# Infini-attention scores on one core: q and k as two fp32r parts, even and odd heads in the two row halves of the array, scores of two heads nine apart issued together

## The chip, the cores and the metric

The kernel runs on one core of a Trainium2 chip. The metric is device time in microseconds (us). TensorE (PE) has a row of its own in the profile for loading its stationary operand (PEld); DVE is VectorE, ACT is ScalarE, POOL is GpSimd, SP is SyncE, which issues most transfers (POOL issues a few).

## The reference

Two independent parts are computed and put side by side. Part A is attention with a compressive memory: 2048 tokens of 576 numbers, 32 heads of 18, in four segments of 512 tokens. Part B is a spectral filter: a 2-D FFT of a 2048 x 576 array, a product with complex weights, and the way back.

```python
q,k,v = x@wq, x@wk, x@wv            # 32 heads of 18, 4 segments of 512
for s in range(4):
    logits = qs @ ks.T * 18**-.5 + mask     # mask: -1e9 where the query is before the key (row < col)
    a_dot = softmax(logits) @ vs
    pq = phi(qs)                            # t+1 or exp(t)
    a_mem = (pq @ M) / (pq @ z + 1e-6)      # M, z: sums over earlier segments
    outs.append(g*a_mem + (1-g)*a_dot)      # g = sigmoid(beta), by head
    M += phi(ks).T @ vs;  z += phi(ks).sum(over tokens)
y_a = concat(outs) @ wo
y_b = irfft2(rfft2(xb) * (w_r + 1j*w_i))
```

## The kernel before

The order of work is written out by hand: Python generators are advanced step by step, and the instructions stand on each engine in the order in which the generators were advanced. The stages follow each other, with some overlap: forward transform of part B, projections, inverse transform, attention.

**Projections** (`projections`, `qk_unit`, `v_unit`). For each of four groups g of 512 tokens (a segment) there are nine units of 128 rows of q and k and four of v. A q/k unit is 14 fp32r matmuls of 512 columns into a PSUM bank pj (line 464). The result leaves as three bf16 parts in a tile sp3: ACT copies the first (line 477), DVE subtracts it from the bank (484), ACT copies the second (488); the third is a DVE subtraction (490) in 18 units, and in the other 18 a matmul with `nid`, the negative identity, takes the second part off inside the bank (492) and ACT copies the rest (493). One transfer per unit stores the tile to qkD in memory (494). Between the units, `pace` inserts butterflies of the transform of part B on DVE; ACT also makes phi of q and k (480, 481), PE transposes it, and sums M and z come from it and v.

**Stacks** (`stack_dmas`). Eight heads of one group make a block n (16 blocks). For each block six transfers bring q parts to a tile Qs (ring of three) and six k parts to a tile Ks (ring of four): 18 rows each, six pieces one under the other. The contraction over these 108 rows is the sum of the six products of parts that matter. The first slot of either ring lies in a tile named x0, which the profile calls x.

**Attention** (`attention`). Its loop has one step t for each of 128 heads. Step t makes the first pass s1 of head t+10 and the second pass s2 of head t. s1 computes the scores with queries as rows, four matmuls for the lower triangle and one with the tile tri that adds the mask, in three banks of the ring s1 (three buffers); DVE takes maxima of them (line 654 and twice line 648). Every four heads `mpath` turns the maxima into rows 108 and 109 of Qs (transpose on PE into mt, ACT copy, a POOL transfer). s2 computes the scores again with keys as rows, now over 110 rows so that the maximum is subtracted, in three banks of the ring s2 (three buffers), and ACT takes the exponential to tiles P. POOL zeroes the triangle of P every four heads (701). Then `pv` (718) multiplies P of four heads by v and a column of ones, four heads beside each other in 32-column groups of the array, in every second step. PSUM has two more banks: pv, and post for the side products.

**Side products** in the same loop: pd (denominators of the memory part, `den`), pn (phi(q) times M, `mem1`), pb (spreading of reciprocals over rows, `mem1` and `combine`) and po (the projection with wo, `oproj`, 15 matmuls in two halves). All take their bank by `bank`:

```python
a="post" if s.now<119 else "s1" if s.now<131 or name=="po" else "s2"
```

They are advanced from one queue `bg` by `run_bg`, at a rate that depends on t modulo 4. `mixed` weaves the combination of group g-1 with the memory part of group g. The functions as they stand before:

## Time and profile before

| | us |
|---|---|
| median of three runs | 712.41 (711.06 to 712.87) |
| span of the profiled execution | 709.2 |
| PE busy | 676.4 |
| PE weight loads busy | 498.7 |
| DVE busy | 556.2 |
| ACT busy | 441.0 |
| POOL busy | 208.8 |

The profiled execution is known by its span, from the first to the last instruction; the runs' median is 3.2 us above it. Busy time is the union of an engine's instructions. Ends of matmuls are modelled, so that they overlap in the list; starts are what tells how fast PE goes. A product of plain f32 operands (pv, pn, pd) shows as two records.

### The profile page before, as it was taken

How to read it: one execution, taken by the hardware profiler on the slowest of the kernel's cores; microseconds unless marked ns; L12 is line 12 of the kernel's file. 1: busy time of each engine (PE TensorE's matmuls, PEld its weight loads, DVE VectorE, ACT ScalarE, POOL GpSimd, SP SyncE). 2: the span in 40 equal slices, each digit the busy share in tenths (PEclk: the TensorE clock that was granted, in tenths of full speed). 3: DMA queues.
4: the chain of work that ended last, by engine and by line, in shares of the span. 5: the costliest groups of instructions: out<-in, count | busy, mean ns of one | idle time of the engine just before them, and what ended most of it. 6: DMA issues, size and time to landing. Idle time of an engine off the chain costs nothing.

```text
span 709.2 us, 14168 instructions
## 1 busy us (share of the span) xinstructions
PE 676.4 (95%) x4861; PEld 498.7 (70%) x4861; DVE 556.2 (78%) x1233; ACT 441.0 (62%) x994; POOL 208.8 (29%) x409
## 2 busy tenths in 40 slices
PE   4999999999999999999999899999999999998997
PEld 4999779889879888999844444444566445764677
DVE  6999999899989889887588688877666876568153
ACT  3657695574574563444388677777666676567741
POOL 2110000100100111565165334555233753246210
PEclk9999999999999999999999999999999999999999
DMA  9876546555563568899647666676556765441331
GB/s 343 272 233 205 150 141 194 175 178 167 165 211 133 165 215 279 201 239 211 180 109 176 172 161 154 173 181 169 128 129 185 171 164 128 122 129 52 99 100 69
DMA packets 83388, 121.04 MB, mean 171 GB/s; under 512 B 11368, under 2 KB 50902, under 8 KB 83180
## 3 DMA queue, kind: packets, MB, share of 16 engines
q1 hardware_dynamic: 76724, 104.11, 51.8%
q0 software_dynamic: 6592, 16.03, 8.2%
q8 instruction: 38, 0.62, 0.4%
q14 instruction: 34, 0.28, 0.1%
HBM read 81.78 MB, written 38.24 MB: 169 GB/s over the span
## 4 chain that ended last, share of the span: by engine, by line
PE 61%; DVE 9%; DMA 6%; ACT 5%; issue 3%; POOL 3%; DVEq 0%; SPq 0%; ACTq 0%; POOLq 0%
PE pv L718 9%; PE po L861 7%; PE pj L464 6%; PE pjv L464 6%; PE s L644 5%; PE i L300 4%; PE i L311 4%; PE s L652 3%; PE s L688 3%; PE po L892 2%; DVE junk L648 2%; PE s L692 2%; PE pn L791 2%; PE pm L524 2%; PE s L653 2%
## 5 line engine op out<-in xcount | busy, mean ns | idle before, releaser
L648 DVE CUSTOM_DVE_ANT_0 junk<-s,mask 128x512 bf16<-128x512 f32 (+1 forms) x256 | 141.8, 554 | 55.1 <-PE s L644 44.3
L654 DVE TENSOR_REDUCE mx<-s 128x4 f32<-128x512 f32 x128 | 87.9, 687 | 20.0 <-PE s L653 18.2
L689 ACT ACTIVATE P<-s 128x512 f32<-128x512 f32 x128 | 77.2, 603 | 24.1 <-PE s L688 20.9
L718 PE MATMUL pv<-P,vs 128*32 128x512 f32 (+3 forms) x1024 | 82.3, 440 | 0.0
L694 ACT ACTIVATE P<-s 128x512 f32<-128x512 f32 x128 | 77.1, 602 | 6.9 <-PE s L693 3.8
L698 ACT ACTIVATE P<-s 128x256 f32<-128x256 f32 x128 | 49.6, 387 | 49.7 <-PE s L697 49.6
L701 POOL TENSOR_SCALAR_AFFINE_SELECT P<-P 128x512 f32<-128x512 f32 x116 | 69.4, 635 | 5.6 <-ACT P L689 4.7
L718 PEld LDWEIGHTS pv<-P,vs 128*32 128x32 f32 x1024 | 26.9, 109 | 45.0 <-issue 42.9
L464 PE MATMUL pj<-x,wqkh 128*128 128x512 f32 x162 | 56.1, 407 | 0.0
L210 DVE TENSOR_TENSOR t<-Z 128x580 f32<-128x580 f32 x64 | 46.7, 757 | 0.2
L514 POOL MEMSET vt<- 128x32 f32 x16 | 2.4, 159 | 148.8 <-PE pm L524 121.5
L210 DVE TENSOR_TENSOR Z<-t 128x580 f32<-128x580 f32 x64 | 45.9, 756 | 0.0
L644 PE MATMUL s<-Ks,Qs 108*128 108x512 bf16 (+1 forms) x128 | 42.2, 330 | 0.0
L488 ACT CAST sp<-pj 128x512 bf16<-128x512 f32 x36 | 21.1, 585 | 30.7 <-DVE pj L484 30.7
L142 PE MATMUL f<-ftab,eh 128*128 128x290 f32 (+1 forms) x160 | 31.6, 317 | 9.0 <-DMA ftab<-ftab 9.0
L300 PE MATMUL i<-civ,Y 128*128 128x256 f32 (+1 forms) x288 | 37.9, 284 | 1.6 <-DVE T L332 1.6
L300 PEld LDWEIGHTS i<-civ,Y 128*128 128x128 f32 (+1 forms) x288 | 35.8, 181 | 1.8 <-DVE T L332 1.8
L311 PE MATMUL i<-itab,T 128*128 128x290 f32 (+1 forms) x224 | 36.4, 312 | 0.0
L464 PEld LDWEIGHTS pj<-x,wqkh 128*128 128x128 f32 x162 | 30.4, 188 | 8.4 <-issue 1.7
L669 POOL CAST mh<-mg 128x16 bf16<-128x16 f32 x32 | 6.8, 214 | 99.1 <-ACT mg L667 67.9
L464 PE MATMUL pj<-xh,wqkh 128*128 128x512 f32 x90 | 35.6, 395 | 0.0
L464 PE MATMUL pj<-xh,wqkl 128*128 128x512 f32 x90 | 35.6, 395 | 0.0
(214 smaller groups left out, 1859.6 us busy)
## 6 DMA issues: line engine op xcount, KB each, us to landing
qkD<-sp SPq DMA_DIRECT2D x36, 384.0 KB
Ks<-qkD SPq DMA_DIRECT2D x72, 144.0 KB
x<-qkD SPq DMA_DIRECT2D x60, 144.0 KB
Qs<-qkD SPq DMA_DIRECT2D x60, 144.0 KB
xin<-xb SPq DMA_DIRECT2D x16, 384.0 KB
cfw<-cfw POOLq DMA_DIRECT2D x16, 384.0 KB, 4.5
civ<-civ POOLq DMA_DIRECT2D x16, 384.0 KB, 7.5
vs<-vD SPq DMA_DIRECT2D x16, 330.0 KB
```

Source lines behind the costliest of these rows:

```text
L210: v.tensor_tensor(o,a,b,op=op)
L300: nc.tensor.matmul(p[:m,k],Y[i][:,q,c*128:c*128+m],cc[:,hl,o:o+256],start=n==0,stop=n==5)
L311: nc.tensor.matmul(p,x,t,start=n==0,stop=n==6)
L464: s.nc.tensor.matmul(out,a,b,start=i==0,stop=i==len(L)-1)
L644: nc.tensor.matmul(out,Q[:108,h,128*i:128*i+128],K[:108,h,:128*(i+1)],start=True,stop=True)
L648: nc.vector.tensor_tensor_reduce(out=junk[:,:w],in0=src,in1=s.mask[:,512-w:],scale=1.0,scalar=-3.0e38, op0=OP.add,op1=OP.max,accum_out=s.m ...
L654: nc.vector.tensor_reduce(out=s.mx[k][:,hh],in_=pa.rearrange("p (b c) -> p b c",c=128),axis=mybir.AxisListType.X,op=OP.max)
L689: nc.scalar.activation(P[0][:,hh],p0,AF.Exp,scale=SC)
L694: nc.scalar.activation(P[1][:,hh],p1,AF.Exp,scale=SC)
L701: if k<29: nc.gpsimd.affine_select(out=x,in_=x,pattern=pat+[[1,128]],compare_op=OP.is_ge,fill=0.0,base=0,channel_multiplier=-1)
L718: nc.tensor.matmul(s.pvt[32*hh:32*hh+32,128*j:],vt[:,j,19*h:19*h+32],mv[0][:,hh,mv[1]],start=j==0,stop=j==2,skip_group_check=True)
L861: nc.tensor.matmul(ps,a[t][:r,c],b[:r,t,w],start=i==0,stop=i==14)
```

## The change

1. A q/k unit leaves as two fp32r parts of 4 bytes, hi (an ACT copy) and lo (a DVE subtraction into SBUF). The matmul with nid, the third part and the second ACT copy go; each part is stored by a transfer of its own. hi shares the buffers of v's output tile (tag hv, three of them), and lo has three.
2. A stack holds four heads in rows 0 to 53 and four in rows 64 to 117: even heads in the lower half of the array's rows, odd heads in the upper. Three products (hi hi, hi lo, lo hi) take 54 rows, and two rows for the maxima make 56. The number of transfers and the bytes per block stay, in rows of 2 KB instead of 1 KB. `mpath` now issues two transfers instead of one, and the constant rows of Ks come by two instead of one.
3. s1 and s2 become `pair(a,b)`: a is nine heads ahead of b, so that the two lie in different halves. The four matmuls of b and the four of a alternate, then comes the mask matmul over all 128 rows. Of DVE's reductions the one for 512 columns now comes first. Before the loop, `two` makes nine heads' maxima, two heads at a time.
4. `bank` gives post to po alone; pn, pb and pd, and mt, take a buffer of the ring s2 (pn, pb and pd post for steps 119 to 130). `mixed` and `run_bg` go: `parts` makes a list of pieces, marked b or n, of which a step takes at most one (b after the scores, n after the value product), and `half` advances the projection po in odd steps and one more in eight.

```diff
+        hi=tp.tile([128,622],F32,name="hv",bufs=3)[:,:512].bitcast(F32R); lo=tp.tile([128,512],F32R,name="lo",bufs=3)
...
-        nc.scalar.copy(sp3[:,0],ps)
+        nc.scalar.copy(hi,ps)
...
+        nc.sync.dma_start(row[:,0],hi.bitcast(F32))
+        nc.vector.tensor_tensor(lo,ps,hi.bitcast(F32),op=OP.subtract)
-        nc.vector.tensor_tensor(ps,ps,sp3[:,0],op=OP.subtract)
...
-        nc.scalar.copy(sp3[:,1],ps)
-        yield
-        if s.third(g,mt): nc.vector.tensor_tensor(sp3[:,2],ps,sp3[:,1],op=OP.subtract)
-        else:
-            nc.tensor.matmul(ps,s.nid,sp3[:,1],start=False,stop=True,skip_group_check=True)
-            nc.scalar.copy(sp3[:,2],ps)
-        nc.sync.dma_start(s.qkD[g][128*mt:128*mt+128],sp3)
+        nc.sync.dma_start(row[:,1],lo.bitcast(F32))
...
-        T,base,order=((s.Qs[n%3],0,(0,0,0,1,1,2)),(s.Ks[n%4],576,(0,1,2,0,1,0)))[qk]
+        T,base,order=((s.Qs[n%3],0,(0,0,1)),(s.Ks[n%4],576,(0,1,0)))[qk]
...
+    def ops1(s,a):
+        k,hh=divmod(a,4); n,h=divmod(a,8); r=64*(h%2)
...
+        Q,K=s.Qs[n%3][r:r+54,h//2],s.Ks[n%4][r:r+54,h//2]
+        return lambda i: (Q[:,128*i:128*i+128],K[:,:128*i+128])
...
+    def pair(s,a,b):
+        nc=s.nc; A=[]; B=[]
+        if b is not None:
+            u,hb=divmod(b,4); o=s.ops2(b); P=s.P[u]
+            p0,p1=[s.ps.tile([128,512],F32,name="s2",tag="s2") for _ in range(2)]; p2=s.ps.tile([128,256],F32,name="s2",tag="s2")
+            B=[(p0,o(0)),(p1[:,:384],o(1)),(p1[:,384:],o(3)),(p2,o(2))]
+        if a is not None:
+            o=s.ops1(a); pc,pa,pb=s.bank1(),s.bank1(),s.bank1(256)
+            A=[(pc,o(3)),(pa[:,:384],o(2),True,False),(pa[:,384:],o(0),False,False),(pb,o(1))]
+        for i in range(4):
+            for L in (B,A):
+                if L: s.mm(*L[i])
+        if A: s.tris(pa)
+        ex=lambda i,p: nc.scalar.activation(P[i][:,hb],p,AF.Exp,scale=SC)
+        if B: ex(0,p0)
+        if A: s.red(a,pc,3)
+        yield
+        if B: ex(1,p1); ex(2,p2)
+        if A: s.red(a,pa,2); s.red(a,pb,1)
...
-        a="post" if s.now<119 else "s1" if s.now<131 or name=="po" else "s2"
+        if name=="po": a="post" if s.now<119 else "s1"
+        else: a="post" if 118<s.now<131 else "s2"
...
+            pr=s.pair(t+9 if t+9<128 else None,t) if t<128 else iter(())
+            next(pr,None)
+            did=part("b")
             r=(t-5)%4
-            if r%2: run_bg(1)
...
+            if 5<=t<129: s.pv((t-5)//4,r)
+            next(pr,None)
+            if not did: part("bn" if t>118 else "n")
...
+            if r%2 or t%8==5 or t>118: half()
```

PE's order in the middle of attention, where one head's scores and a value product stand; before, each bf16 matmul has its weight load as an instruction of its own, s2 is lines 688 to 697 and s1 is lines 644 to 653:

```order
L688 LDWEIGHTS Ks_3180
L688 MATMUL s_6605<-Qs_3176,Ks_3180 128x512
L644 LDWEIGHTS x_2655
L644 MATMUL s_6608<-Ks_3178,x_2655 128x512
L692 LDWEIGHTS Ks_3180
L692 MATMUL s_6612<-Qs_3176,Ks_3180 128x384
L693 LDWEIGHTS Ks_3180
L693 MATMUL s_6612<-Qs_3176,Ks_3180 128x128
L718 MATMUL pv<-P_6325,vs 32x384 x4
L718 MATMUL pv<-P_6326,vs 32x256 x4
L644 LDWEIGHTS x_2655
L644 MATMUL s_6624<-Ks_3178,x_2655 128x256
```

The value product stands between the scores of a step there. After, PE's order at such a step (line 644 is now the one helper for all score matmuls, whose fp32r weight loads are no instructions of their own, and line 727 is the value product):

```order
L644 MATMUL s_6701<-Qs_3153,x_2637 128x512
L644 MATMUL s_6704<-Ks_3154,x_2637 128x512
L644 MATMUL s_6702<-Qs_3153,x_2637 128x384
L644 MATMUL s_6705<-Ks_3154,x_2637 128x384
L644 MATMUL s_6702<-Qs_3153,x_2637 128x128
L644 MATMUL s_6705<-Ks_3154,x_2637 128x128
L644 MATMUL s_6703<-Qs_3153,x_2637 128x256
L644 MATMUL s_6706<-Ks_3154,x_2637 128x256
L644 LDWEIGHTS idb
L644 MATMUL s_6705<-tri,idb 128x256
L727 MATMUL pv<-P_6470,vs 32x512 x4
L727 MATMUL pv<-P_6471,vs 32x128 x4
```

All nine matmuls of a step now stand in one row, pairs of equal size beside each other, and the value product behind them. PE's order where side products stand, before:

```order
L697 MATMUL s_6589<-Qs_3176,Ks_3180 128x256
L674 LDWEIGHTS mh
L674 MATMUL mt<-idb,mh 128x128
L797 LDWEIGHTS sel
L797 MATMUL pb<-rd,sel 126x512
L652 LDWEIGHTS x_2655
L652 MATMUL s_6600<-Ks_3178,x_2655 128x384
```

and after, in the step that is followed by the one shown above:

```order
L644 MATMUL s_6661<-tri,idb 128x256
L807 LDWEIGHTS sel
L807 MATMUL pb<-rd,sel 126x512
L712 LDWEIGHTS mh
L712 MATMUL mt<-idb,mh 128x128
L863 MATMUL po<-woh,oh 128x288 x4
L863 MATMUL po<-wol,oh 128x288 x4
L644 MATMUL s_6701<-Qs_3153,x_2637 128x512
```

pb and mt take two of the three buffers of s2 here, and a half of po follows in its own bank, ahead of the next step's scores. ACT's order in the projections, before:

```order
L477 CAST sp_1588<-pj 128x512
L480 ACTIVATE ex<-pj 128x512
L481 ACTIVATE ex<-ex 128x512
L488 CAST sp_1588<-pj 128x512
L477 CAST sp_1638<-pj 128x512
L480 ACTIVATE ex<-pj 128x512
```

and after:

```order
L477 CAST hv<-pj 128x512
L480 ACTIVATE ex<-pj 128x512
L481 ACTIVATE ex<-ex 128x512
L498 COPY pk<-ptr 128x4x128
L477 CAST hv<-pj 128x512
L480 ACTIVATE ex<-pj 128x512
```

The second copy of a unit (line 488) is gone from between the units.

More of the change, by code (lines that the diff above doesn't have):

```diff
@@ L396, in __init__ @@
         d=lambda n,sh,dt: dp.tile(sh,dt,name=n)
-        s.qkD=[d(f"qkD{i}",[1152,3,512],BF) for i in range(4)]
+        s.qkD=[d(f"qkD{i}",[1152,2,512],F32) for i in range(4)]
         s.pqD=[None]+[d(f"pqD{i}",[576,512],F32) for i in range(1,4)]
@@ L465, in passes @@
             if i==6 and not swap: yield
-    def third(s,g,mt): return g>0 and mt%3
     def qk_unit(s,g,mt,tp,pp):
@@ L928, in attention @@
     def attention(s,tp,ps):
-        nc=s.nc; s.tp,s.ps,s.psm,s.mtag=tp,ps,s.ps1,"s1"
+        nc=s.nc; s.tp,s.ps,s.psm,s.mtag=tp,ps,ps,"s2"
         s.homes()
-        def steps(gen,i):
-            for _ in range(i):
-                try: next(gen)
-                except StopIteration: return
         m=None
@@ L937, in attention, with part, half @@
         qu=[]
-        bg=[s.late_setup(tp)]
-        state=dict(acc=0.0)
-        def run_bg(rate):
-            state["acc"]+=rate
-            if state["acc"]>=1:
-                state["acc"]-=1
-                while bg:
-                    try: next(bg[0]); break
-                    except StopIteration: bg.pop(0)
+        setup=s.late_setup(tp); M=[]; R=[]
+        def part(kinds):
+            while M and M[0][0] in ("go","x"):
+                x,c=M.pop(0)
+                if x=="go": R.append(c)
+                else: next(c,None)
+            if M and M[0][0] in kinds: next(M.pop(0)[1],None); return True
+        def half(n=1):
+            for _ in range(n):
+                while R:
+                    try: next(R[0]); break
+                    except StopIteration: R.pop(0)
         lane=[]
@@ L1006, in attention @@
             if qu: qu.pop(0)()
-            run_bg((.3,1,.5,1)[r])
+            if t>118: part("bn"); half()
             s.due(t)
@@ L1012, in attention @@
         i=0
-        while bg or i<9:
+        while M or R or i<9:
             for l in list(lane):
@@ L1016, in attention @@
                 except StopIteration: lane.remove(l)
-            run_bg(1.0)
+            part("bn"); half()
             i+=1
```

203 lines of the change are left out of this document (88 added, 115 removed).

## Prediction, made before the changed kernel was run

> **What bounds the kernel now.** First the page's busy times: TensorE (PE) leads.
>
> ```profile
> PE 676.4 (95%) x4861; PEld 498.7 (70%) x4861; DVE 556.2 (78%) x1233; ACT 441.0 (62%) x994; POOL 208.8 (29%) x409
> ```
>
> Then busy time by stage: projections, inverse transform, three parts of attention, and the last projection.
>
> ```profile
> 99.00:275.00 176.00, 174.03 (x1027) 152.28 (x1026) 161.76 (x257) 104.21 (x215) 14.76 (x62) 1.00 0.57 186
> 275.00:350.70 75.70, 74.05 (x577) 70.31 (x577) 56.77 (x131) 33.19 (x82) 34.77 (x52) 1.00 0.81 208
> 350.70:457.90 107.20, 100.80 (x844) 49.27 (x842) 88.17 (x269) 80.99 (x197) 50.71 (x97) 0.98 0.65 159
> 457.90:647.10 189.20, 182.93 (x1454) 104.56 (x1452) 133.79 (x380) 127.92 (x302) 82.88 (x148) 1.00 0.57 144
> 647.10:674.20 27.10, 25.74 (x221) 15.88 (x219) 11.11 (x21) 21.48 (x51) 11.63 (x15) 1.00 0.31 93
> 674.20:709.20 35.00, 31.19 (x223) 26.92 (x222) 15.84 (x25) 9.56 (x21) 2.68 (x6) 0.99 0.26 85
> ```
>
> Columns: length, busy us of PE, weight loads (PEld), DVE, ACT, POOL, then PE's granted clock (0.98 to 1.00, so no throttle matters below), the transfers' share and GB/s. I cut attention at the first score matmul (line 688) of heads 0, 50 and 117. Part A (heads 0 to 49) has 107.2/50 = 2.14 us a head, part B (50 to 116) 189.2/67 = 2.82. In B PE is busy 97%, DVE 71%, ACT 68%: PE bounds B. In A PE has 94% and DVE 82%.
>
> The timeline of PE shows one head:
>
> ```profile
> 436.34 0.38 PE L688 MATMUL s<-Qs,Ks 110*128 110x512 bf16 x1
> 436.56 0.38 PE L644 MATMUL s<-Ks,x 108*128 108x512 bf16 x1
> 436.78 0.33 PE L692 MATMUL s<-Qs,Ks 110*128 110x384 bf16 x1
> 436.94 0.22 PE L693 MATMUL s<-Qs,Ks 110*128 110x128 bf16 x1
> 437.00 0.27 PE L644 MATMUL s<-Ks,x 108*128 108x256 bf16 x1
> ...
> 437.50 0.27 PE L653 MATMUL s<-tri,idb 128*128 128x256 bf16 x1
> 437.62 0.38 PE L688 MATMUL s<-Qs,Ks 110*128 110x512 bf16 x1
> ...
> 438.42 1.28 PE L718 MATMUL pv<-P,vs 128*32 128x512 f32 x16
> 439.64 0.28 PE L644 MATMUL s<-Ks,x 108*128 108x256 bf16 x1
> ```
>
> Starts count, since ends are modelled. A 512-column matmul takes 0.22 us, 384 columns 0.16, 128 columns 0.06, the mask matmul of line 653 0.12; nine of them make a head of 437.62-436.34 = 1.28 us. Every second head has the value product (line 718) too, 439.64-438.42 = 1.22, so 0.61 a head.
>
> DVE's timeline for one head:
>
> ```profile
> 432.13 0.69 DVE L654 TENSOR_REDUCE mx<-s 128x4 f32<-128x512 f32 x1
> 432.74 0.68 DVE L648 CUSTOM_DVE_ANT_0 junk<-s,mask 128x512 bf16<-128x512 f32 x1
> 433.35 0.08 DVE L648 DVE_READ_ACCUMULATOR2_ANT mg<- 128x1 f32 x1
> 433.57 0.42 DVE L648 CUSTOM_DVE_ANT_0 junk<-s,mask 128x256 bf16<-128x256 f32 x1
> 433.92 0.08 DVE L648 DVE_READ_ACCUMULATOR2_ANT mg<- 128x1 f32 x1
> 434.01 0.69 DVE L654 TENSOR_REDUCE mx<-s 128x4 f32<-128x512 f32 x1
> ```
>
> From reduce to reduce 434.01-432.13 = 1.88 us. The change keeps these three reductions, so attention can't fall under about 1.88 a head. In A, 1.28+0.61 = 1.89 is already there, and the rest is waiting; in B PE has 2.82-1.89 = 0.93 of side products and waits.
>
> **The change, part by part.** *Scores.* Contraction rows fall from 108/110 to 54/56, and two heads lie in rows 0-63 and 64-127, so the eight score matmuls go as four pairs. If the halves overlap, a pair costs one matmul. No row of before has two row halves at work; the nearest is the value product, whose four heads lie in four column groups. Its loads start together, and in the chain of waits one 512-column f32 product alone (two records) takes 1.12:
>
> ```profile
> 430.08 0.16 PEld L718 LDWEIGHTS pv<-P,vs 128*32 128x32 f32 x8 [0.21 <-issue]
> 480.91 1.12 PE pn L791 x2
> ```
>
> Four of those in a row would be over 4 us; the whole block takes 1.22. So parts of the array do overlap, by columns at least. The dtype becomes fp32r. Its rate is in the chain's rows of the projections and the inverse, its loads in the groups by line:
>
> ```profile
> 134.38 9.80 PE pj L464 x42
> 291.07 1.41 PE i L300 x12
> L464 PEld LDWEIGHTS pj<-x,wqkh 128*128 128x128 f32 x162 | 30.4, 188 | 8.4 <-issue 1.7
> ```
>
> 9.80/42 = 0.233 for 512 columns, 1.41/12 = 0.118 for 256: one column costs as in bf16, and though a load has 188 ns, it hides down to 0.118 a matmul. A 128-column fp32r matmul is in no row; I take the 0.118 at which loads still hid. Pairs: 0.22+0.16+0.12+0.12, mask 0.12, sum 0.74.
>
> Passing between array layouts costs too. The value product follows a 128-column matmul by 0.14 instead of 0.06:
>
> ```profile
> 429.94 0.22 PE L693 MATMUL s<-Qs,x 110*128 110x128 bf16 x1
> 430.08 1.28 PE L718 MATMUL pv<-P,vs 128*32 128x512 f32 x16
> ```
>
> so 0.08 a change. The mask matmul keeps all 128 rows, so a head gets two new changes, 0.16. That gives 0.90 a head. The bounds: 0.74 if changes are free, and with no overlap 2x(0.233+0.175+0.118+0.118)+0.12 = 1.41 (384 columns taken in proportion), 1.57 with the changes. I take 0.90, by the overlap in the value product. The Trainium skill, "TensorEngine Tiling (Array Packing)", section Key Properties, says that a change of tiling mode drains the TensorE; it speaks against this layout, the 0.08 agrees with it, and a sum that ignored it would be 0.16x67 = 11 us lower.
>
> *Part A.* PE would need 0.90+0.61 = 1.51, DVE 1.88; DVE becomes the bound. Six score banks are all taken by one head, so neither engine runs far ahead, and heads come at DVE's pace: 50x1.88 = 94. One wait there is for transfers, as the chain shows:
>
> ```profile
> 390.54 6.15 DMA Ks<-qkD
> ```
>
> Packets double to 2 KB at equal bytes, which should help a little; I leave 3 us. 107.2-97 = 10 saved.
>
> *Part B.* 0.90+0.61+0.93 = 2.44 on PE. DVE's busy time in B was 133.79; in the head shown above it was busy from 432.13 to 433.43 and from 433.57 to 434.00, 1.73, and 67x1.73 = 116, so side products took it 18, or 0.27 a head, and 1.88+0.27 = 2.15 is its bound: below PE's.
>
> ```profile
> L798 DVE TENSOR_TENSOR am<-am,pb 126x512 f32<-126x512 f32 (+1 forms) x10 | 6.8, 682 | 0.0
> ```
>
> The side products pn, pb, pd and the transpose mt now take turns in the ring s2 of three banks, which each head wants whole; a pn has to be copied out by ACT, a pb multiplied on DVE (0.68) behind the first reduction, before the next head's third score finds its bank. The other side: "post" is left to the output projection alone. Between nothing and 0.38 a head (then all is lost) I take 0.08, since in B most heads have an output-projection half (7 to 8 matmuls) to run meanwhile. 67x(2.82-2.52) = 20 saved.
>
> *After head 118* only one head is in a pair: nothing changes there, nor in the last 35 us. The lead falls from ten heads to nine: one head's maxima move into the loop, under steps that DVE passed half idle (11.11 of 27.10); nothing. In the inverse nine heads instead of ten, each now with layout changes: nothing either way, within 2 us.
>
> *Projections.* Removed: 18 matmuls with nid, 36 and 18 ACT copies, 18 DVE subtractions; a second transfer is added to each of 36 units.
>
> ```profile
> 144.18 0.23 PE pj L492
> L492 PE MATMUL pj<-sp,nid 128*128 128x512 bf16 x18 | 6.9, 384 | 3.0 <-ACT sp L488 2.5 <-DVE t L210 0.4
> L490 DVE TENSOR_TENSOR sp<-pj,sp 128x512 bf16<-128x512 f32 x18 | 12.3, 684 | 0.0
> L488 ACT CAST sp<-pj x36: 572/585/597, 79.5 to 264.6; 128x512 bf16<-128x512 f32 x36
> L493 ACT CAST sp<-pj x18: 562/577/612, 80.6 to 259.9; 128x512 bf16<-128x512 f32 x18
> qkD<-sp SPq DMA_DIRECT2D x36, 384.0 KB
> L678 POOL DMA_DIRECT2D Qs<-mts x20 | 12.3, 613 | 29.7 <-ACT mts L677 29.5 <-ACT P L694 0.2
> ```
>
> PE loses 18x0.23 = 4.1 and 3.0 of idle time before them: 7. DVE loses 12.3 of 161.8, so the transform's steps that fill it don't become the bound; ACT loses 36x0.585+18x0.577 = 31, which PE waited for only in those 3.0. Of the 7 I count 6, since a unit sends 512 KB to qkD instead of 384 and the buffer hv is now shared with v. SP issues 36 more transfers; behind them queue only other stores and loads of inputs wanted a group of tokens later, and PE doesn't wait: nothing, and if it did, what the 6 leaves off. POOL issues 32 more transfers of maxima and 4 more constants, 0.61 us each, 22 us on an engine at 29%; the selects behind them are due two heads later; without that cover a value product would wait 0.61.
>
> Sum: 10+20+6 = 36 us. 709.2-36 = 673; the runs' median is 712.4, 3.2 above the span, so 676.
>
> **The rivals.**
> 1. *The halves don't overlap* (the change doesn't do what it says). For it: no row shows row halves. Against: column groups do. PE then has 1.41 to 1.57 a head: in B 0.13 to 0.29 more, 9 to 19 us; in A 1.57+0.61 = 2.18 against 2.14, 0 to 2; projections -6. 715 to 728, slower. It decides from 1.37 a head: there B loses the projections' 6 us.
> 2. *The s2 ring eats part B.* Each of the side products holds a bank that the next head's third score needs, and PE, in order, stops there. For it: one ring, 3 buffers, a DVE multiply behind a reduction. Against: today the same products share one bank with the output projection, and PE is still busy 97% of B. B stays at 2.82: 712.4-10-6 = 696.
> 3. *DVE bounds everything.* Layout changes and side waits vanish, B runs at 2.15: 67x0.67 = 45 instead of 20, so 712.4-10-45-6 = 651. For it: nothing on DVE goes but the projections' part. Against: the 0.08 above, and side products that stand behind the value product in one head and are missing in the next.
>
> **How the numbers follow.** Forecast 0.63 (660 to 690), rival 1 0.12, rival 2 0.14, rival 3 0.11. The first, second and fourth of these are faster: 0.88, less 0.01 for something unseen; of rival 1 0.02 ends within 0.3% (some 2 us, about what a measurement tells from no change), 0.10 beyond, so same 0.03 and slower 0.10. The range reaches up over rival 2 with its size unsure, to 704, and leaves rival 1 out; down to about rival 3's 651, cutting half of it.
>
> **What would show it.** On PE two score matmuls should start within a few hundredths of each other and pairs 0.22 apart; from a head's first score to its mask's end about 0.9. DVE should be busy over 90% in A with heads near 1.9 us, and B near 2.5. In the projections no nid, and ACT some 30 us less. It is wrong if scores start one after the other at 0.2, or if PE waits long for copies of pn or pb.

## The result and the profile after

The changed kernel takes 740.64 us (median of 4 runs, 736.37 to 742.88) against 711.73 in the same session: 1.0394 times as long, 95% interval 1.0343 to 1.0445. The forecast was 676, in a range from about 651 to 704, with a chance of 0.87 for faster. It was wrong in sign. Runs of a kernel more than 1.5% above its fastest count as slow: they are in the medians of e4_noalt, e7_lead10, e8_spread and e9_spread_tail below, and the stages of e7_lead10 and e8_spread come from one, while the ratios go by the other runs.

The page's busy times after, and its row of TensorE's granted clock in 40 slices of the span (tenths, 9 is 0.9 and more):

```profile
PE 689.2 (93%) x4843; PEld 517.2 (70%) x4843; DVE 543.0 (73%) x1213; ACT 415.7 (56%) x939; POOL 230.0 (31%) x447
...
PEclk9999999999999999999698999799989999998989
```

PE still leads, 13 us busier than before. Before, the clock row has a 9 in every slice; now it dips in slices 20, 22, 26, 30 and behind, and the mean granted clock fell from 0.997 to 0.963. The same windows as in the prediction, cut at the first exponential of heads 0, 50, 117 and 127 (length; busy PE, PEld, DVE, ACT, POOL; clock; transfers' share; GB/s):

```profile
99.00:275.00 176.00, 175.30 (x1055) 156.19 (x1054) 158.27 (x249) 86.88 (x177) 18.35 (x72) 1.00 0.64 212
275.00:345.40 70.40, 70.36 (x526) 64.61 (x524) 50.02 (x116) 29.92 (x75) 35.40 (x53) 1.00 0.81 203
345.40:459.30 113.90, 104.79 (x844) 57.25 (x842) 86.37 (x270) 81.75 (x197) 56.79 (x109) 0.91 0.58 151
459.30:659.10 199.80, 185.53 (x1452) 108.55 (x1449) 130.90 (x380) 126.25 (x302) 91.39 (x163) 0.96 0.53 139
659.10:702.40 43.30, 39.87 (x253) 28.27 (x253) 14.78 (x26) 22.38 (x50) 12.51 (x17) 0.92 0.17 50
702.40:739.90 37.50, 25.84 (x191) 21.67 (x190) 14.27 (x22) 8.86 (x20) 4.54 (x9) 0.87 0.24 77
```

With the same cuts in the trace of before (start of head 0 at 351.2, then A 107.2, B 189.2, the last ten heads, here C, 23.2, the rest 38.4) the span's 30.7 us come from: start -5.8 (the projections' gain, as forecast), A +6.7, B +10.6, C +20.1, the rest -0.9. Against the forecast, A is off by 17, B by 31 and C by 20.

One undisturbed pair of heads, PE's timeline after:

```profile
509.41 0.49 PE L644 MATMUL s<-Qs,x 56*128 56x512 f32 x1
509.41 0.50 PE L644 MATMUL s<-Ks,x 54*128 54x512 f32 x1
509.75 0.33 PE L644 MATMUL s<-Qs,x 56*128 56x384 f32 x1
509.75 0.34 PE L644 MATMUL s<-Ks,x 54*128 54x384 f32 x1
509.92 0.22 PE L644 MATMUL s<-Qs,x 56*128 56x128 f32 x1
509.93 0.22 PE L644 MATMUL s<-Ks,x 54*128 54x128 f32 x1
509.98 0.33 PE L644 MATMUL s<-Qs,x 56*128 56x256 f32 x1
509.99 0.33 PE L644 MATMUL s<-Ks,x 54*128 54x256 f32 x1
510.25 0.28 PE L644 MATMUL s<-tri,idb 128*128 128x256 bf16 x1
510.46 1.29 PE L727 MATMUL pv<-P,vs 128*32 128x512 f32 x16
```

The halves do overlap: rows 0-63 and 64-127 start within 0.01 us. But the steps are 0.34, 0.17, 0.06, 0.27 and 0.21, 1.05 in all, where the forecast had 0.90 and the kernel before 1.28. The last 0.21 is the time from the mask matmul to the start of the value product. In steps without a value product (the even ones; there, and not in odd steps, `half` runs, since its r counts from t-5) a half of the projection po can come next, and then the nine take 0.87 (621.54 to 622.41 in the same trace).

In part A, DVE's first maximum of a head waits for PE where a value product stood ahead of the scores:

```profile
449.52 0.83 PE L727 MATMUL pv<-P,vs 128*32 128x512 f32 x12
...
450.85 0.69 DVE L653 CUSTOM_DVE_ANT_0 junk<-s,mask 128x512 bf16<-128x512 f32 x1 [0.58 <-PE s L644]
```

What each kind of matmul took of PE's time (from its start to the next start, less idle time, summed over the trace's records; B1 is heads 50 to 83, B2 84 to 116; mt, pb, pn and pd are left out):

| us | scores | pv | po | idle | total |
|---|---|---|---|---|---|
| A before / after | 68.9 / 68.6 | 28.3 / 31.2 | - | 6.4 / 8.9 | 107.2 / 113.9 |
| B1 before / after | 43.8 / 41.2 | 20.7 / 24.9 | 17.9 / 20.5 | 3.0 / 8.5 | 95.9 / 105.9 |
| B2 before / after | 41.9 / 38.8 | 19.5 / 19.6 | 18.0 / 19.5 | 3.2 / 5.8 | 93.3 / 93.9 |

In B2, where the clock is whole, scores take 38.8/33 = 1.18 a head, 3 us less than before; the added idle time and slower po take that back. In B1 pv, which the change doesn't touch, takes 20% more: there the clock is at half for 17.1 us.

### The profile page after: what moved, and what is told of

The parts are those of the page before. It is cut to its first block, busy times and chain, and to the rows that moved or that the text cites. A ratio compares the mean times of both kernels' runs of the same rounds, so it can differ in the third digit from the quotient of the medians.

```text
span 739.9 us, 14199 instructions
## 1 busy us (share of the span) xinstructions
PE 689.2 (93%) x4843; PEld 517.2 (70%) x4843; DVE 543.0 (73%) x1213; ACT 415.7 (56%) x939; POOL 230.0 (31%) x447
## 4 chain that ended last, share of the span: by engine, by line
PE 68%; DMA 7%; ACT 4%; issue 3%; DVE 3%; POOL 2%; SPq 0%; ACTq 0%; DVEq 0%; POOLq 0%
PE s L644 14%; PE pj L464 13%; PE pv L727 8%; PE pjv L464 8%; PE po L863 6%; PE i L300 5%; PE i L311 4%; ACT P L686 3%; PE po L894 2%; PE pn L801 2%; DMA Qs<-mts 2%; DMA x<-qkD 2%; PE pm L519 2%; DMA x<-mts 1%; PE ptr L496 1%
## 5 line engine op out<-in xcount | busy, mean ns | idle before, releaser
L686 ACT ACTIVATE P<-s 128x512 f32<-128x512 f32 (+1 forms) x384 | 176.4, 528 | 48.8 <-PE s L644 48.1
L727 PE MATMUL pv<-P,vs 128*32 128x512 f32 (+3 forms) x1024 | 89.6, 471 | 0.1
L644 PE MATMUL s<-Qs,Ks 56*128 56x512 f32 (+3 forms) x256 | 65.3, 365 | 6.8 <-ACT P L686 3.3
L644 PE MATMUL s<-Ks,Qs 54*128 54x512 f32 (+3 forms) x256 | 68.1, 373 | 1.3 <-DVE mx L650 1.1
L644 PEld LDWEIGHTS s<-Qs,Ks 56*128 56x128 f32 x256 | 42.8, 190 | 32.9 <-issue 13.5
L644 PEld LDWEIGHTS s<-Ks,Qs 54*128 54x128 f32 x256 | 44.8, 196 | 7.2 <-PE s L644 2.8
L477 ACT CAST hv<-pj 128x512 fp32r<-128x512 f32 x36 | 21.1, 587 | 50.6 <-PE pj L464 49.1
L708 POOL CAST mh<-mg 128x16 bf16<-128x16 f32 x32 | 6.6, 206 | 112.7 <-DVE mg L705 61.6
L644 PE MATMUL s<-x,Ks 56*128 56x512 f32 (+3 forms) x128 | 32.1, 364 | 7.0 <-ACT P L686 4.2
L300 PE MATMUL i<-civ,Y 128*128 128x256 f32 (+1 forms) x288 | 37.6, 282 | 0.7 <-DVE T L332 0.7
L644 PE MATMUL s<-tri,idb 128*128 128x256 bf16 x128 | 36.8, 293 | 0.0
L464 PE MATMUL pj<-x,wqkl 128*128 128x512 f32 x90 | 35.6, 395 | 0.0
```

The source lines that it names most:

```text
L300: nc.tensor.matmul(p[:m,k],Y[i][:,q,c*128:c*128+m],cc[:,hl,o:o+256],start=n==0,stop=n==5)
L464: s.nc.tensor.matmul(out,a,b,start=i==0,stop=i==len(L)-1)
L644: def mm(s,out,ab,start=True,stop=True): s.nc.tensor.matmul(out,ab[0],ab[1],start=start,stop=stop,skip_group_check=True)
L686: ex=lambda i,p: nc.scalar.activation(P[i][:,hb],p,AF.Exp,scale=SC)
L727: nc.tensor.matmul(s.pvt[32*hh:32*hh+32,128*j:],vt[:,j,19*h:19*h+32],mv[0][:,hh,mv[1]],start=j==0,stop=j==2,skip_group_check=True)
```

## The experiments

First reading of the trace: PE waited for late transfers of maxima and for the ring s2, idled, and was then put at half clock; past head 118 side products are advanced twice a step. Rival: the two-half fp32r work itself. The table has all results (e12_lead10_spread_128 was run twice, the others four times); half is the time at half clock in that stage, in the profiled run; A, B1, B2 and C as above, tail from head 127 on.

| kernel | median us | ratio to before, 95% | start | A (half) | B1 (half) | B2 (half) | C (half) | tail |
|---|---|---|---|---|---|---|---|---|
| before | 711.7 | 1 | 351.2 | 107.2 (3.4) | 95.9 (0) | 93.3 (0) | 23.2 (0) | 38.4 |
| after | 740.6 | 1.034-1.045 | 345.4 | 113.9 (20.5) | 105.9 (17.1) | 93.9 (0) | 43.4 (6.8) | 37.5 |
| e1_early | 743.9 | 1.039-1.049 | 345.2 | 112.6 (17.1) | 104.1 (13.7) | 96.1 (3.4) | 44.7 (17.1) | 38.7 |
| e2_tail | 734.5 | 1.027-1.038 | 345.3 | 116.1 (20.5) | 100.5 (10.2) | 94.4 (3.4) | 33.6 (6.8) | 40.6 |
| e3_banks | 767.8 | 1.074-1.084 | 346.3 | 115.3 (20.5) | 115.4 (17.1) | 106.4 (6.8) | 42.5 (6.8) | 38.9 |
| e4_noalt | 758.2 | 1.057-1.069 | 344.6 | 125.6 (30.7) | 104.7 (13.7) | 96.7 (3.4) | 43.3 (6.8) | 37.5 |
| e7_lead10 | 817.5 (804-824) | - | 346.1 | 163.7 (99.0) | 116.3 (17.1) | 111.5 (13.7) | 40.7 (6.8) | 38.8 |
| e8_spread | 768.1 | 1.064-1.081 | 345.7 | 126.8 (34.1) | 111.1 (17.1) | 101.6 (3.4) | 43.5 (6.8) | 38.9 |
| e9_spread_tail | 762.2 | 1.066-1.079 | 346.2 | 120.9 (17.1) | 105.2 (3.4) | 103.0 (6.8) | 37.1 (13.7) | 40.9 |
| e10_lead10_spread | 992.2 | 1.387-1.404 | 345.8 | 188.5 (169.5) | 187.1 (165.0) | 181.5 (162.7) | 45.7 (18.2) | 38.9 |
| e11_rows | 741.3 | 1.036-1.051 | 350.0 | 113.1 (13.7) | 105.6 (17.1) | 93.9 (0) | 43.3 (6.8) | 38.9 |
| e12_lead10_spread_128 | 764.2 | 1.066-1.085 | 357.9 | 126.8 (3.4) | 104.3 (0) | 101.1 (0) | 36.1 (0) | 37.3 |
| e13_rows_early_tail | 734.9 | 1.028-1.043 | 352.8 | 112.7 (17.1) | 97.7 (3.4) | 94.5 (3.4) | 34.3 (10.2) | 40.6 |
| e15_split128 | 732.1 | 1.022-1.035 | 360.8 | 109.9 (0) | 99.5 (0) | 97.8 (0) | 24.3 (0) | 38.8 |
| e16_fill | 739.1 | 1.030-1.045 | 348.5 | 113.8 (6.8) | 103.2 (13.7) | 94.4 (3.4) | 43.5 (6.8) | 37.6 |
| e17_tail_memlate | 738.2 | 1.030-1.042 | 344.7 | 118.7 (27.3) | 105.3 (17.1) | 94.2 (3.4) | 30.7 (6.8) | 44.5 |
| e18_fill_tail_memlate | 735.9 | 1.026-1.042 | 346.9 | 113.8 (3.4) | 104.4 (17.1) | 94.6 (3.4) | 34.7 (20.5) | 44.6 |
| e19_fill_even | 744.7 | 1.047-1.055 | 348.3 | 116.3 (6.8) | 102.4 (10.2) | 93.8 (0) | 43.4 (6.8) | 37.5 |
| e20_fill_even_tail | 742.1 | 1.040-1.048 | 347.0 | 115.6 (10.2) | 103.4 (13.7) | 95.0 (3.4) | 33.6 (6.8) | 40.6 |
| e21_lead10_128 | 761.0 | 1.068-1.077 | 357.8 | 121.3 (0) | 104.6 (0) | 101.0 (0) | 36.6 (0) | 37.7 |

**Late maxima.**

```diff
-            if t%4==0 and m is not None:
+            if t%4==3 and m is not None:
```

> The kernel after, with the maxima's transpose and transfers finished one head earlier (end of steps 3, 7, 11... instead of 4, 8, 12...), nothing else. Theory (late maxima: the first score of a group waits for their landing, TensorE idles some us, and then runs at half clock): the periods at half clock inside the loop shrink from about 44 us to under 25, part A falls from 113.9 to about 105, and the whole from 740.6 to 721 to 731. Rival (the clock falls because two halves of fp32r work draw more, not because of idling): the half-clock periods stay and the time is within 3 us of 740.6. Rival (side products' bank holds the same step up anyway): waits move to the transpose, and the time is within 5 us.

From the list of PE's waits in part A (us in total, times, longest), after and then with this edit:

```profile
PE s L644 <- ACT P L686: 2.7, 10, 0.3
PE s L644 <- DMA Qs<-mts: 2.3, 2, 1.8
```
```profile
PE s L644 <- ACT P L686: 4.4, 11, 0.8
PE s L644 <- DMA Qs<-mts: 1.0, 1, 1.0
```

The waits for transfers halved, those for exponentials (ACT, line 686) grew by 1.7 us, and the time didn't fall: 743.9, with A 1.3 us shorter where 9 were forecast. Late transfers are not what the kernel loses by; the theory falls.

**The doubled rate past head 118.**

```diff
-            if t>118: part("bn"); half()
```

> The kernel after, without the second call for side products and output projection in each step past head 118; what isn't done by then falls to the closing loop, as in the kernel before. Theory (the doubled rate put side products between the last heads and left nothing to run under the last reciprocals): heads 117 to 127 take about 28 us instead of 43.3, the rest behind grows by at most 4, and the whole falls to 724 to 731. Rival (the work is only moved): the last heads are 10 to 15 us shorter, the stretch behind them as much longer, and the whole is within 3 us of 740.6.

6 us gained, less than the 10 to 17 of the theory: C lost 9.8, the tail took back 3.1. Behind the last head one wait of after is gone in this kernel, that for the transfer of the last reciprocals:

```profile
PE pb L873 <- DMA rr<-rrD: 5.1, 1, 5.1
```

The chain of waits of after shows what C still holds (around head 118, then a step of a single head):

```profile
662.85 0.23 issue
663.08 0.69 DVE ux L837
663.78 0.02 issue
663.80 2.26 DVE am L838
666.06 0.60 DVE ol L822
666.66 0.61 DVE mx L650
...
668.50 0.51 ACT P L686
669.01 0.04 issue
669.05 1.11 PE s L644 x3
...
680.36 0.93 PE po L863 x7
681.29 0.83 PE s L644 x4
682.12 1.05 PE pn L801 x2
683.17 1.06 PE po L863 x8
684.23 0.22 PE pb L807
```

For 6 us (662.85 to 669.05) the chain lies mostly on combine steps on DVE that stand ahead of the maxima, and on ACT behind them; PE stands idle for 3.4 us of these (0.63, 2.26 and 0.51 in its timeline), and half clock begins at 668.5. And a step of one head has 0.83 of scores (before, by the chain's rows there, 0.22+0.18+0.06+0.11 = 0.57), with pn, po and pb in every step.

**The banks.** Old banks in the new loop; since po can be half done in the shared bank, it is closed first.

```diff
-        if name=="po": a="post" if s.now<119 else "s1"
-        else: a="post" if 118<s.now<131 else "s2"
+        a="post" if s.now<119 else "s1" if s.now<131 or name=="po" else "s2"
...
+                if s.po and s.now<119: half()
```

> The kernel after with the side products' banks as in the kernel before: pn, pb, pd (and mt in the first heads) in the bank of the output projection, which is closed first when a half of it is open, and the later mt in the ring s1. Theory (side products in the ring s2 hold up the next head's scores by some us in each step that has one): part B falls from 199.8 to 185 to 195 and the whole to 726 to 736. Rival (one bank for both costs as much, by waits on the copy of po): within 4 us of 740.6, or slower.

27 us slower than after, 22 of it in B in the profiled runs. In this loop the new banks are a gain over the old ones, and the theory falls. What the ring s2 costs by itself this run doesn't show. PE's waits for exponentials to free a buffer of it, in B of after, are:

```profile
PE mt L712 <- ACT P L686: 2.3, 4, 0.6
PE s L644 <- ACT P L686: 1.9, 3, 0.8
PE pb L807 <- ACT P L686: 1.5, 4, 0.4
PE pd L781 <- ACT P L686: 0.8, 2, 0.4
```

That is 6.5 of the 14.3 us that PE is idle in B; in the list of B before, no wait of PE is for an exponential.

**Order within a pair.**

```diff
-        for i in range(4):
-            for L in (B,A):
-                if L: s.mm(*L[i])
+        for L in (B,A):
+            for x in L: s.mm(*x)
```

> The kernel after, with the four transposed scores of one head issued first and then the four of the other, so that neighbours lie in the same row half but for one passage. Theory (alternating halves do overlap, and part B is bound by TensorE): a head's scores take 1.4 instead of 1.05 us, part B grows by 0.3 to 0.4 a head, 20 to 27 us, part A by under 10, the whole to 760 to 775. Rival (waits set the pace and the overlap is worth nothing): within 5 us of 740.6.

B hardly moved (+1.6), and its trace says why: although one head's four matmuls are now issued ahead of the other's, they still start in twos where nothing waits (head's own time 1.09):

```profile
635.41 0.49 PE L644 MATMUL s<-x 56*128 56x512 f32 x1
635.47 0.47 PE L644 MATMUL s<-Ks,Qs 54*128 54x512 f32 x1
635.75 0.34 PE L644 MATMUL s<-x 56*128 56x384 f32 x1
635.77 0.33 PE L644 MATMUL s<-Ks,Qs 54*128 54x384 f32 x1
```

So this edit didn't undo the overlap, and that the whole came near the forecast (758.2 against 760 to 775) was luck: the loss is in A, 11.7 us, with 10 us more at half clock, and not in B.

**Same row half, and spread scores.** A lead of ten puts both heads in one half; the other edit issues the scores in three pieces with the side product and pv between.

```diff
-            pr=s.pair(t+9 if t+9<128 else None,t) if t<128 else iter(())
+            pr=s.pair(t+10 if t+10<128 else None,t) if t<128 else iter(())
```

> The kernel after with a lead of ten heads instead of nine: both heads of a pair have the same parity and lie in the same row half, so their matmuls can't run beside each other; ten heads in the prologue, the maxima's first step one head earlier, their transfers where they were. Theory (the row halves' overlap does shorten TensorE's work by some 0.35 us a head, and the loss lies elsewhere): scores take 1.4 to 1.5 us a head where they took 1.05, part B grows by 15 to 25 us, part A by 5 to 12, the whole is 760 to 780. Rival (the row halves gain nothing because each step waits for ACT and DVE): within 6 us of 740.6.

```diff
-        for i in range(4):
-            for L in (B,A):
-                if L: s.mm(*L[i])
-        if A: s.tris(pa)
+        go(0)            # exp of p0, maximum of pc, then a piece b
...
+        go(1,2)          # mask; exp of p1, maximum of pa, then pv
...
+        go(3)            # exp of p2, maximum of pb, then a piece n
```

> The kernel after with a pair's scores issued in three pieces, as the kernel before spread them (first the two of 512 columns, then a side product, then those of 384 and 128 and the mask, then the value product, then those of 256), each with its own exponential and maximum behind it. Theory (all three score banks of a head are asked for at once, so TensorE stands until the last exponential of the head before, idles in many steps and drops to half clock): idle time in B falls from 14 us by half, half-clock time from 56 us to under 30, and the whole to 715 to 730. Rival (the side products in the ring s2 are what holds it, whatever the order): within 5 us of 740.6. Rival (each return from row halves to the whole array costs 0.08 and more, and there are now three a head): slower, 745 to 760.

> Both the spread scores and the single rate past head 118. Theory: the two gains add, the second about 6 us as it was alone (740.6 to 734.5): 708 to 724, that is, no slower than the kernel before or close to it. Rival (spread scores gain nothing): 730 to 738.

> The kernel after with a lead of ten (no row halves beside each other) and with the scores spread over the step: what is left of the change is the two fp32r parts, the buffers, the banks and the new side schedule. Theory (the spread is what matters, the overlap some 0.35 us a head beside it): slower than the spread kernel with row halves by 10 to 25 us. Rival (with the scores spread the overlap is worth nothing, since one bank at a time is asked for): within 4 us of the spread kernel.

With a lead of ten the time is 817 us, beyond the forecast's 780: A alone grew by 50 us, with 99 us at half clock. Its runs spread too widely for a ratio. Every spread kernel was slower (768, 762 and 992), not faster, so spreading the scores in this way is no cure; what the three pieces cost isn't shown. The last one, at 992 us, fits neither its theory nor its rival and is the key. From head 0 to 117 its windows row reads:

```profile
345.80:903.00 557.20, 556.29 (x2292) 321.31 (x2291) 232.19 (x651) 225.97 (x499) 152.81 (x275) 0.55 0.32 81
```

PE is busy 99.8% and yet granted 0.55 of its clock. So the clock can be halved without idling. What these kernels share is that a score matmul uses 54 of 128 rows, and here no second one runs beside it.

**Rows.** The new theory: work in rows times columns. Two kernels, one with the rows of after raised to 62 and 64 (zeros, maxima moved to 62, 63, 126, 127), the other the 992 us kernel over all rows.

```diff
-        Q,K=s.Qs[n%3][r:r+54,h//2],s.Ks[n%4][r:r+54,h//2]
+        Q,K=s.Qs[n%3][r:r+62,h//2],s.Ks[n%4][r:r+62,h//2]    # e11, e13
+        Q,K=s.Qs[n%3][:126,h//2],s.Ks[n%4][:126,h//2]        # e12
...
-        q,kk=s.Qs[n%3][r:r+56,h//2],s.Ks[n%4][r:r+56,h//2]
+        q,kk=s.Qs[n%3][r:r+64,h//2],s.Ks[n%4][r:r+64,h//2]
+        q,kk=s.Qs[n%3][:128,h//2],s.Ks[n%4][:128,h//2]
```

> The kernel with a lead of ten and spread scores (992 us, TensorE never idle, half clock in 529 us), but each score matmul now runs over all 128 rows (126 for the maxima), so that the two parities of a pair of heads are summed: this leaves out the separation of even and odd heads, and the output isn't attention's. Same number of matmuls, columns and order. Theory (the clock follows rows times columns of work): full clock nearly throughout, scores 1.6 us a head, 735 to 775. Rival (fp32r scores or the many changes of layout make the clock fall, or more rows draw more current): 970 or more. Rival (in part a matter of idling): between 800 and 950.

764 us. The same stage:

```profile
357.90:690.10 332.20, 317.17 (x2292) 211.05 (x2291) 219.60 (x650) 209.80 (x498) 150.09 (x273) 0.99 0.53 135
```

The same 2292 matmul records, in the same order and with the same columns, take 332 us instead of 557, at clock 0.99. More rows did it, or what goes with them: over all rows no score matmul lies in a half of the array, so the changes between a half and the whole are gone too, and this pair of runs doesn't part the two. The fp32r scores by themselves are ruled out, since e12 has them. Two things speak for the rows: the extra matmuls over all rows further down leave those changes as they are and lower the half clock in A, and the count of windows in the last section goes by rows, while by the number of such changes it finds nothing.

> The kernel after with every score matmul 62 or 64 rows deep instead of 54 or 56: eight rows of each half are set to zero once and the maxima stand in rows 62, 63 and 126, 127. Same matmuls, same columns, same order, seven buffers more to clear on POOL before attention. Theory (the clock is halved after a window of 3.41 us in which rows times columns of work come to less than about 0.37 of what the array could do, and the change took half of the scores' rows away): about as many microseconds at full clock a head, but windows under 0.37 fall from 15 to 6 to 11, half-clock time from 56 us to 25 to 40, and the whole from 740.6 to 725 to 735. Rival (the clock follows only how long TensorE idles): half-clock time and total stay, 737 to 744.

> The 64-row scores with the maxima finished one head earlier and the single rate past head 118. Theory (with the clock held, the waits that these two take away count): the 64-row kernel less 6 for the tail and 0 to 5 for the transfers, 715 to 728. Rival (the two change nothing more): as the 64-row kernel alone, less 6.

Eight more rows in each half were too few: half-clock time fell from 56 to 51 us and not to 25 to 40, the time (741.3) is the rival's, and clearing the buffers put the start 4.6 us later. By the count of the last section, windows under the limit fell from 15 to 13, not to 6 to 11; the limit held, the forecast of the number didn't. With the two earlier edits B1 falls to 97.7, but the total (734.9) is no lower than with the tail edit alone, as the rival has it.

**The split alone, and overlap without the clock.** e15_split128 is the kernel before (its loop, lead, banks and side schedule) with the two fp32r parts over all rows. e21_lead10_128 is the new loop with a lead of ten (the edit above) over all rows (as e12).

```diff
-            nc.tensor.matmul(out,Q[:108,h,128*i:128*i+128],K[:108,h,:128*(i+1)],start=True,stop=True)
+            nc.tensor.matmul(out,Q[:126,h//2,128*i:128*i+128],K[:126,h//2,:128*(i+1)],start=True,stop=True)
...
-        q=lambda o: Q[:110,h,o:]
+        q=lambda o: Q[:,h//2,o:]
...
```

> The kernel before with only the new split: q and k as two fp32r parts (projections, stores, v buffers as after), two transfers of maxima, but the old loop, lead, banks and side schedule, and each score matmul over all 128 rows (126 for the maxima), which sums even and odd heads: this leaves their separation out, and the output isn't attention's. Theory (the split itself is worth the projections' 6 us, fp32r scores cost at most 0.1 us a head more, and the rows keep the clock up): 702 to 712. Rival (fp32r in the scores costs by itself): 720 or more.

> The kernel with a lead of ten (both heads of a pair in the same row half, 817 us), with its score matmuls over all 128 rows (126 for the maxima), which sums the two parities: this leaves their separation out, and the output isn't attention's. Nothing overlaps and the clock should hold, so it gives the price of the overlap without the clock. Theory (half clock was most of the 77 us by which the lead of ten was slower, and overlap at full clock is worth the difference of 1.6 and 1.05 us a head in B, 30 to 37 us, with little in A): half-clock time from 150 to under 30 us, the whole 755 to 780 with some 5 us of buffers to clear. Rival (overlap is worth little once the clock holds): 735 to 750.

Their stages from head 0 to 117, first e15_split128, then e21_lead10_128:

```profile
360.80:668.00 307.20, 300.55 (x2293) 212.27 (x2292) 221.73 (x650) 210.74 (x499) 150.03 (x274) 1.00 0.57 145
```
```profile
357.80:684.60 326.80, 312.60 (x2292) 217.90 (x2291) 223.87 (x650) 216.13 (x498) 149.56 (x272) 1.00 0.52 137
```

Both hold the clock, with fp32r scores, and have the same matmuls without overlap; their late starts (buffers are cleared first, and half clock falls into the inverse transform) are left out below. The first forecast (702 to 712) was missed: 732.1, of which the start takes 9.6 us more than before and the loop 11.9, or 0.09 a head. The second (755 to 780) held: 761.0. From head 0 to 127 (A, B1, B2, C added): before 319.6; the split in the old loop 331.5, +11.9; the new loop, banks and side schedule 363.5, +32.0; rows 0-63 beside 64-127, with 54 rows and their half clock, 357.1, -6.4. The 32.0 is by far the largest term. One undisturbed head in the new loop without overlap:

```profile
625.06 0.40 PE L646 MATMUL s<-x 128*128 128x512 f32 x1
625.29 0.39 PE L646 MATMUL s<-Ks,Qs 126*128 126x512 f32 x1
...
626.35 0.28 PE L646 MATMUL s<-tri,idb 128*128 128x256 bf16 x1
626.56 1.28 PE L729 MATMUL pv<-P,vs 128*32 128x512 f32 x16
```

That is 1.50 a head, against 1.05 with overlap. Of these 0.45, B2 (no half clock in either) shows (101.0-93.9)/33 = 0.22.

**Filling the gaps, and C once more.**

```diff
+            if t<50: s.mm(<a buffer of post>,(s.idb,<tri, four times>))               # e16, e18
+            if t<58 and t%2==0: s.mm(<a buffer of post>,(s.idb,<tri, four times>))    # e19, e20
...
-            if M and M[0][0] in kinds: next(M.pop(0)[1],None); return True
+            if M and M[0][0] in kinds and not (118<s.now<131 and <a piece marked n or of mem1>): next(M.pop(0)[1],None); return True    # e17, e18
```

> The kernel after with one extra matmul of 512 columns and 128 rows (0.22 us, bf16) ahead of each of the heads 0 to 49, into the bank of the output projection, which is unused there; nobody reads it. Theory (in part A DVE sets the pace at 2.01 a head, so TensorE has room for it, and its rows lift the windows that fell under 0.37 of the array's work): half-clock time in A falls from 20 us to under 7, part A from 113.9 to 103 to 109, the whole from 740.6 to 728 to 737. Rival (half clock in A costs nothing because DVE bounds it): part A stays at 112 to 116. Rival (TensorE bounds A): A grows by the 50x0.3, to 125 to 130.

> The kernel after with the single rate past head 118, and the memory products pn and pb of the last group held back until the last value product, as they mostly were in the kernel before. Theory (in the last ten heads TensorE did side products that used to fill the wait for the last reciprocals): heads 117 to 127 fall to 25 to 30 us (33.6 with the single rate alone, 43.3 after, 23.2 before), the stretch behind grows by under 4, the whole from 734.5 to 726 to 732. Rival (the rest of the loss there is the combine step and half clock): within 3 us of 734.5.

> The extra matmuls in part A together with the two changes past head 118. Theory: the gains add, 714 to 728. Rival (the extra matmuls are worth nothing): as the two changes alone.

> The kernel after with the extra matmul of 512 columns and 128 rows only ahead of the even heads from 0 to 56, whose steps have no value product and in which TensorE waited for DVE (with one ahead of every head, undisturbed groups of four grew from 8.07 to 8.68). Theory (half clock costs about 0.57 us for each of its us in a stage that TensorE bounds, and work in these gaps lifts the windows): undisturbed groups stay near 8.1, half-clock time in A and the first 34 heads of B falls from 38 us to under 20, A to 106 to 111, the first 34 heads of B to 97 to 103, the whole from 740.6 to 724 to 734. Rival (the gaps aren't free, or the low windows come from waits longer than 0.22 us can lift): within 4 us of 740.6.

> The same with the single rate past head 118. Theory: 6 us less than the former, 718 to 728. Rival: as the single rate alone, 734.

The fill cut half clock in A from 20.5 to 6.8 us, and A stayed. But undisturbed groups of four heads took 8.68 instead of 8.07, with four fills as with two, so it cost 0.61x12.5 = 7.6 us over A. An estimate from this: 13.7 us less of half clock gave about 7.6 back, 0.55 for each; the three other kernels with fills give 0.4 to 0.6 in the same way. Holding the memory products back moved work behind the last head (C 30.7, tail 44.5), and at 738.2 it gained nothing over the tail edit; why isn't shown. The fills together with the tail edits missed their forecasts too: 735.9 and 742.1. No version beats the kernel before; the best of those that leave nothing out takes 734.5.

## Why the prediction was wrong, step by step

- **Projections, -6.** Right: head 0 starts 5.8 us earlier, the matmul with nid is gone, and ACT's second and third copies, 31 us, with it.
- **"If the halves overlap, a pair costs one matmul"; 0.90 a head.** The overlap is there, and rival 1 is refuted; without it a head takes 1.50, inside the 1.41 to 1.57 given. The size was off: 1.05 ahead of a value product. The pair of 512 columns takes 0.34, where e21's one matmul over all rows takes 0.23, and the pair of 256 up to the mask 0.27, where one takes 0.13. That is 0.11 and 0.14 more at the two changes of layout, which the sum had at 0.08 each (an estimate: the trace doesn't part a matmul from the change beside it). In B2 the scores take 1.18 on average, since one half sometimes waits for a bank while the other runs, and since pb or mt behind the mask can wait for a buffer. This is 33x0.28 = 9 us of B2's miss of 93.9-33x2.52 = 10.7.
- **"DVE becomes the bound", 1.88 a head in A.** Wrong. Undisturbed groups of four take 8.05 to 8.09 after and 7.80 or 8.34 before, so in such groups A was already near the pace that the forecast hoped for, and it runs at 2.01 a head, not 1.88. DVE, forecast busy over 90% of A, is busy 76%. It isn't the only bound: behind a value product it stands idle for PE's next scores (0.58 us at 450.85), and extra matmuls on PE lengthened the undisturbed groups (8.07 to 8.68). So PE's time counts in A too.
- **"No throttle matters below."** This step had no rival. It took the clock of before for granted while the change halved the rows, and with them the work of each column. In ten kernels with the order of after for heads 50 to 83, B1 follows half-clock time: 97.7 us at 3.4, 100.5 and 102.4 at 10.2, 103.2 to 104.1 at 13.7, 104.4 to 105.9 at 17.1. The line through them rises by 0.56 us for each us and stands at 95.8 at none, the time before. So B1's loss of 10 goes with the clock. But the clock isn't the whole miss: at no half clock B1 and B2 (93.9 against 93.3) are as long as before, and the forecast had each some 10 us shorter. An estimate for heads 0 to 127: 44.4 us at half clock, at 0.56 each, are 25 us; without them the kernel would take 332 us there, and the kernel before takes 319.6.
- **The new loop, its banks and its side schedule, counted at next to nothing** (0.08 a head for waits in the ring, in B only). This is the largest failed term: between the two kernels at full clock it costs 32 us, 11.4 in A, 8.3 in B, 12.3 in C. Which part of it costs what stays open.
- **Rival 2, the ring s2.** Not settled. With the old banks B is 22 us longer, so the old banks were no way out; but PE waits 6.5 us in B for buffers of the ring, and without half clock B would be as long as before, which is what this rival gave.
- **"After head 118 ... nothing changes there."** False: C is 20 us longer, the stretch behind it 0.9 shorter. The doubled rate is 6 (shown by taking it away). Counted as in the table of matmuls, from head 117 to the end PE's idle time grew from 1.4 to 10.3 us (5.1 of it the wait for the last reciprocals), scores by 4.1 and po by 3.1, half clock included; these shares are read from the trace and weren't tested apart.
- **POOL's extra transfers, the lead of nine.** The transfers cost nothing that showed: moving them a head earlier didn't shorten the time. The lead of nine wasn't tested apart.

## What to carry to other kernels

A change that leaves a matmul's columns and takes its rows away can lose by the clock what it wins in work: before counting on it, compare the rows times columns of each few microseconds with those of the kernel before, the slowest stages first. When a gain is worked out for one engine, ask of each stage whether that engine bounds it in undisturbed steps, and give the new order of the loop a price of its own, with a kernel that has the new order and nothing else.

## What the runs showed of the hardware

**The clock follows work, rows included.** Half clock comes in pieces of 3.41 us. In the changed kernel, at the start of attention:

```profile
347.70:351.10 3.40, 3.18 (x20) 1.76 (x18) 3.25 (x11) 2.61 (x7) 0.00 (x0) 1.00 0.90 242
351.10:354.50 3.40, 3.40 (x18) 2.07 (x16) 2.66 (x11) 2.65 (x7) 3.04 (x8) 0.50 0.12 34
...
361.30:364.70 3.40, 3.40 (x25) 1.51 (x22) 2.24 (x9) 2.12 (x5) 2.65 (x6) 0.50 0.17 40
364.70:368.10 3.40, 2.97 (x31) 1.70 (x27) 2.44 (x8) 2.81 (x7) 2.25 (x4) 1.00 0.22 36
```

PE was busy 3.18 of 3.40 us, and half clock followed for four windows. To see what sets it I counted for each 3.41 us window of the loop in all 20 traces its matmuls' moving columns, times the share of 128 rows and of 128 columns in use (two passes for each record of a plain f32 product), and divided by 8192, about what a window holds at 0.21 us for 512 columns. So 1 is an array that is full all the time. The four windows from 347.7 to 361.3 have 0.31, 0.26, 0.35 and 0.34, the next one 0.38, and full clock is back. Over all traces, windows under 0.37 are followed by half clock and others by full clock, whatever their own clock: 41 of 2176 windows are on the wrong side. The limit stands in the expectation of e11_rows, which knew the first ten traces of the table; of the 1028 windows of the later ten, 15 are on the wrong side. Without the share of rows at least 201 of 2176 are, by busy time 331, and by the number of changes between a half and the whole array 370, as many as are followed by half clock at all. That it is a rule of the chip, and not only of these kernels, isn't shown. The mean of the windows is 0.74 before, 0.54 after, 0.32 in the 992 us kernel and 0.72 in the same kernel over all rows. No window at half clock reached more than 0.48, so a stage of 54-row matmuls stays down long: the 992 us kernel's work, done in the 332 us of the same kernel over all rows, would come to 0.32x557/332 = 0.54 a window (an estimate), above the limit, but at half clock it stays at 0.32, below it. The Trainium skill, "TensorE: Matmul & The Clock Gate", section "Part 1: The HAM clock gate (the 'warmup' mystery)", has the window of about 3.4 us and says that half clock comes after an idle one. The window's length agrees. Idleness isn't needed here, as PE's 99.8% at clock 0.55 shows; the measurement decides.

**Two row halves run side by side in both orders of issue tried** (starts 0.01 us apart with the halves in turn, 0.06 us apart with three other matmuls issued between them), as long as neither waits for a bank.
